# Attention, MLP and capacity MoE on one core: the turned product with v for five more pairs, and later stores and splits

## The chip, the cores and the metric

The kernel runs on 1 core of one Trainium2 chip, in one launch. The metric is the device time of that launch in microseconds (us), the median of several executions. TensorE is PE in the profile (PEld is its weight load), VectorE is DVE, ScalarE is ACT, GpSimd is POOL, and SyncE, which issues nearly all DMAs, is SP.

## The reference

Three stages follow each other. The change touches the first and the way in which weights of the second are prepared.

```python
# attention: 4 batches, 12 heads, 448 tokens, head size 64
q_n, k_n = rmsnorm(q, g_q), rmsnorm(k, g_k)
scores = q_n @ k_n.T / 8
attn = exp(scores - max(scores)); attn = attn / (sum(attn) + 1e-9)
x = attn @ v                       # to 1792 tokens x 768
# hardswish MLP, 768 -> 2048 -> 768; its weights arrive as 64-bit floats
h = x @ w_in;  g = h * clip(h + 3, 0, 6) / 6;  x = g @ w_out
# MoE: 8 experts of 224 tokens each, tokens assigned by capacity
out = relu(x @ w1[e]) @ w2[e]
```

## The kernel before, in words

Attention works on pairs of heads: 24 pairs, numbered i = 0 to 23, six of them (NP) to a batch. The order of all work is written out by hand: each piece is an event with a time in steps, 16 steps to a pair (`at(t + T_..., function, i)` with t = 16 i, near line 720), and the events are recorded in the order of these times. Between the events pieces of the first MLP product (`h`, L520) are laid in, but only once a batch is complete; so between the pairs of the first batch there are none, and the attention stands alone there.

The steps of a pair that matter here, with their lines:

- `sums`, `invert`, `norm` (L240 to L269): squares on ACT (`sq`), their sums on DVE (`st`, L249), the inverse root for two pairs at a time in 11 small DVE operations (L253 to L258), and the two scaled operands `xn` on POOL.
- `transp` (L286 to L298): PE turns `xn`; ACT and DVE make a high and a low part (`qh`, `kh`, `ql`, `kl`).
- `s1` (L309): scores for the maximum; DVE reduces them (`mx`, L312); `mt` (L318, L320) turns the maxima and DVE spreads them as `mr`.
- `sT` (L331): the turned scores minus the maximum; ACT takes the exponential into `ph` (L342).
- The product with v comes in two forms. `av` (L371) keeps queries on the rows: 32 small products of 66 columns for a pair, whose 65th column is the sum; DVE copies the sums (`scol`, L386), ACT the rest (`num`, L387), POOL divides (`normalize`, L392), and `xt` (L403 to L405) turns the result on PE and splits it on ACT and DVE. `pv` (L420) gives the turned result at once: 8 products of 448 columns. Its sums need more: `padd` (L413) adds blocks of `ph` in pairs on POOL, four operations of 448 columns; `psums` (L429) sums them on PE; the sums go out to memory, come back in another shape, are inverted on DVE (L444), go out again and come back spread over 64 rows (`rs_out`, `rs_in`, `r_out`, `r_in`, L435 to L454, five DMAs on SP); then POOL multiplies (`xmul`, L458), ACT takes the high part and POOL the low part (`xsplit`, L466 and L468).

The table `QMAJOR` names the pairs that use `av`. Within a pair I call A(i) the first score block (`sT` of parts 0 and 1, with `s1` parts 2 and 3 of pair i + 1) and B(i) the second (`sT` of parts 2 and 3, with `s1` parts 0 and 1 of pair i + 2).

`conv` (L147 to L171) narrows the 64-bit weights in 128-row units, 16 of `w_in` (one every 10 steps from step 20 on) and then 16 of `w_out` (one every 12 steps from step 180 on): one ACT operation (L138) and three DVE operations (L139 to L141) into the one buffer `cv`, then a store on SP (L171 for `w_in`, L169 for `w_out`). All PSUM tiles share eight banks under one tag, and every engine works its instructions off in the order in which they are recorded.

Of the kernel before, what the change touches and what calls it, by code (L numbers as in the profile page):

```python
# [21 lines left out]
def kernel(  # L22
# [15 lines left out]
    B, H, S, D = q.shape  # L38
# [7 lines left out]
    NP = H // 2  # L46
# [27 lines left out]
    T_AV = ((17, 18, 19.5, 20.5), (22, 23, 24.5, 25.5))  # L74
    T_NUM, T_XT, T_MLP = 28, 33, (37, 41, 41, 37)
    T_ADD, T_PV, T_SUM = (6, 13), (15.6, 15.62, 15.64, 15.66), 15.7
    T_RS, T_RL, T_REC, T_RO, T_RB, T_X, T_XH, T_XL = 19.5, 21.5, 24, 25.5, 28, 33, 35.5, 39.5
    GD, WD2, C_ST = 12, 8, 5
    QMAJOR = tuple(range(NP)) + (B * NP - 1,)
    T_CI, D_CI, T_CO, D_CO, T_CL = 20, 10, 180, 12, 14  # L80


# [52 lines left out]
    def narrow(lo, hi, v):  # L135

        vi = v.bitcast(I32)
        return (lambda: nc.scalar.activation(v, hi.bitcast(F32), AF.Copy, scale=2.0 ** -112),  # L138
                lambda: nc.vector.tensor_scalar(vi, vi, 3, None, op0=OP.logical_shift_left),  # L139
                lambda: nc.vector.scalar_tensor_tensor(vi, lo, 29, vi, op0=OP.logical_shift_right, op1=OP.bitwise_or),  # L140
                lambda: nc.vector.scalar_tensor_tensor(vi, hi, -2147483648, vi, op0=OP.bitwise_and, op1=OP.bitwise_or))  # L141
# [5 lines left out]
    def conv(key, part):  # L147

        out_, n = key
        rows = slice(n * 128, (n + 1) * 128)  # L150
        if part < 0:
            raw = rawp.tile([128, 768, 2], I32, name="wraw", bufs=2)
            if out_:
                nc.sync.dma_start(raw.rearrange("p f t -> p (f t)"), w_out.bitcast(I32)[rows, :])
            else:
                nc.sync.dma_start(raw.rearrange("p (c f) t -> p c (f t)", c=NC),
                                  w_in.bitcast(I32)[:, n * 256:(n + 1) * 256].rearrange("(c p) f -> p c f", p=128))
            RAW[key] = raw
            return
        if part == 0:  # L160
            raw = RAW[key]
            v32 = rawp.tile([128, 768], F32, name="cv", bufs=CB)
            RAW[key] = (v32, narrow(raw[:, :, 0], raw[:, :, 1], v32))
        v32, steps = RAW[key]
        if part < 4:
            steps[part]()
        elif part == C_ST:
            if out_:
                nc.sync.dma_start(wo32[rows, :], v32)  # L169
            else:  # L170
                nc.sync.dma_start(w32[:, rows].rearrange("(c p) f -> p c f", p=128), v32.rearrange("p (c f) -> p c f", c=NC))  # L171
# [551 lines left out]
    def at(t, fn, *args):  # L723
        events.append((t, len(events), fn, args))
# [7 lines left out]
    for i in range(NH // 2):  # L732
        t = 16 * i
# [11 lines left out]
        for c in range(NCH):  # L745
            at(t + (T_S1[c] if i else -24 + 0.1 * c), s1, i, c)
            at(t + T_ST[c], sT, i, c)
            if i in QMAJOR:
                for s in range(2):
# [3 lines left out]
        at(t + (T_MT if i else -21), mt, i)  # L753
        if i in QMAJOR:
            at(t + T_NUM, normalize, i)
# [13 lines left out]
    for u in range(NF if wide else 0):  # L769
        for out_, t in ((0, T_CI + D_CI * u), (1, T_CO + D_CO * u)):  # L770
            at(t - T_CL, conv, (out_, u), -1)
            for part in (0, 1, 2, 3, C_ST):
                at(t + part, conv, (out_, u), part)
    events.sort(key=lambda e: e[:2])
    ENDS = [8 * H * (b + 1) - 16 + T_MLP[b] for b in range(B)]
    now = 0
# [554 lines left out]
```

## Time and profile before

| | |
|---|---|
| median of 3 runs | 1217.49 us (1215.24 to 1219.66) |
| profiled execution, its own time | 1219.53 us |
| its span in the profile | 1217.7 us |
| mean granted TensorE clock | 0.978 |
| busy over the span | PE 94%, DVE 64%, ACT 45%, POOL 40% |
| chain that ended last | PE 62%, DVE 14%, DMA 9%, issue 6%, ACT 4%, POOL 2% |

The busy share is a mean over stages with different limits: attention with the first MLP product fills about the first 550 us, the rest belongs to the second MLP product, the routing and the experts. A line of the timeline gives start, length, engine, line, operation, output and inputs, how many were merged, and in brackets the idle time before with what ended it.

### The profile page before, as it was taken

The page shows a single profiled execution, that of the slowest core. Times are in us where ns is not written, and L with a number is a line of the kernel's source. Part 1 is how long each engine was busy: PE and PEld are TensorE (multiplying, and loading weights), DVE is VectorE, ACT ScalarE, POOL GpSimd, SP SyncE. Part 2 cuts the span into 40 slices and gives each one's busy share as a digit, 9 for nine tenths or more (in the row PEclk, how much of TensorE's full clock was granted, in tenths as well). Part 3 has the DMA queues.
Part 4 walks back from the last instruction along what each step waited for, and adds up shares of the span by engine and source line. Part 5 has one row for each costly group of instructions (what it writes and reads, how often), then busy time and mean ns, then how long its engine had stood idle before and what let it go on. Part 6 is the DMA issues. An engine that isn't in the chain of part 4 may idle for free.

```text
span 1217.7 us, 19761 instructions
## 1 busy us (share of the span) xinstructions
PE 1145.3 (94%) x7204; PEld 931.2 (76%) x7204; DVE 780.7 (64%) x1580; ACT 552.1 (45%) x1019; POOL 490.6 (40%) x362
## 2 busy tenths in 40 slices
PE   3988999999999999999979999999998799999997
PEld 2877656667676677787758787777778799999997
DVE  7887977767657665346893466666676675555550
ACT  3655646555454555446663111111123566555650
POOL 2222554754345432112352222222243677666640
PEclk9888999999999999999999999999999899999999
DMA  4355998977786866649895222222234688778731
GB/s 127 116 163 144 261 303 255 302 273 242 236 279 214 277 223 241 211 149 321 261 298 157 61 75 66 79 57 65 79 100 129 203 257 263 229 235 240 230 116 45
DMA packets 210708, 230.84 MB, mean 190 GB/s; under 512 B 24338, under 2 KB 183732, under 8 KB 210612
## 3 DMA queue, kind: packets, MB, share of 16 engines
q1 hardware_dynamic: 207284, 218.58, 58.3%
q0 software_dynamic: 3328, 11.01, 3.0%
q8 instruction: 56, 0.92, 0.3%
q14 instruction: 40, 0.33, 0.1%
HBM read 178.57 MB, written 50.98 MB: 189 GB/s over the span
## 4 chain that ended last, share of the span: by engine, by line
PE 62%; DVE 14%; DMA 9%; issue 6%; ACT 4%; POOL 2%; SPq 1%; POOLq 0%; DVEq 0%; ACTq 0%
PE y L1135 16%; PE h L520 10%; PE y L1283 8%; PE h L1219 5%; PE st L331 4%; PE av L420 3%; PE av L371 3%; PE h L1221 2%; PE sm L429 2%; PE rt L945 2%; DMA gr<-g_dr 1%; DMA wo_s<-wo 1%; PE s L309 1%; DVE C L940 1%; DMA we_s<-in_moe_w_dram 1%
## 5 line engine op out<-in xcount | busy, mean ns | idle before, releaser
L520 PE MATMUL h<-xh,w 128*128 128x448 f32 x768 | 240.3, 381 | 0.6 <-DVE mr L320 0.3
L520 PEld LDWEIGHTS h<-xh,w 128*128 128x128 f32 x768 | 144.8, 192 | 30.6 <-issue 14.3
L1078 POOL TENSOR_TENSOR g2l<-gr,g2h 128x512 fp32r<-128x512 f32 x60 | 79.1, 1319 | 207.1 <-ACT g2h L1076 159.8
L520 PE MATMUL h<-xl,w 128*128 128x448 f32 x384 | 145.7, 379 | 0.0
L312 DVE TENSOR_REDUCE mx<-s 112x1 f32<-112x448 f32 x192 | 105.9, 612 | 54.2 <-PE s L309 54.1
L1076 ACT ACTIVATE g2h<-gr 128x512 fp32r<-128x512 f32 x60 | 37.9, 631 | 207.1 <-PE y L1135 157.5
L1135 PE MATMUL y<-woh,g2l 128*128 128x512 f32 (+1 forms) x448 | 128.7, 349 | 1.0 <-POOL g2l L1078 1.0
L1135 PE MATMUL y<-woh,g2h 128*128 128x512 f32 (+1 forms) x448 | 128.1, 349 | 0.0
L1135 PE MATMUL y<-wol,g2h 128*128 128x512 f32 (+1 forms) x448 | 126.4, 346 | 0.0
L116 DVE TENSOR_TENSOR wel<-we_s,weh 128x768 fp32r<-128x768 f32 x59 | 80.6, 1372 | 61.5 <-ACT weh L115 59.2
L115 ACT ACTIVATE weh<-we_s 128x768 fp32r<-128x768 f32 x107 | 88.9, 842 | 59.3 <-DMA we_s<-in_moe_w_dram 41.1
L116 POOL TENSOR_TENSOR wel<-we_s,weh 128x768 fp32r<-128x768 f32 x48 | 95.5, 1991 | 46.7 <-ACT weh L115 36.0
L342 ACT ACTIVATE ph<-st 112x448 f32<-112x448 f32 x192 | 93.0, 544 | 46.9 <-PE st L331 46.0
L413 POOL TENSOR_TENSOR pa<-ph 112x448 f32<-112x448 f32 x68 | 85.8, 1282 | 53.6 <-ACT ph L342 53.4
L1219 PE MATMUL h<-xe,weh 128*128 128x448 f32 x318 | 101.4, 378 | 2.2 <-DVE xe L1170 2.2
L520 PEld LDWEIGHTS h<-xl,w 128*128 128x128 f32 x384 | 73.9, 192 | 10.8 <-issue 4.5
L1135 PEld LDWEIGHTS y<-woh,g2l 128*128 128x128 f32 x448 | 73.0, 190 | 10.9 <-POOL g2l L1078 1.3
L1135 PEld LDWEIGHTS y<-woh,g2h 128*128 128x128 f32 x448 | 73.0, 190 | 10.6 <-issue 1.4
L1135 PEld LDWEIGHTS y<-wol,g2h 128*128 128x128 f32 x448 | 72.6, 190 | 9.9 <-issue 0.2
L1221 PE MATMUL h<-xe,wel 128*128 128x224 f32 x318 | 77.2, 270 | 0.0
L1283 PE MATMUL y<-weh,hl 128*112 128x384 f32 x216 | 72.9, 338 | 0.0
L1283 PE MATMUL y<-weh,hh 128*112 128x384 f32 x216 | 72.8, 337 | 0.0
(256 smaller groups left out, 2493.4 us busy)
## 6 DMA issues: line engine op xcount, KB each, us to landing
we_s<-in_moe_w_dram SPq DMA_DIRECT2D x128, 384.0 KB
w<-w_hl SPq DMA_DIRECT2D x32, 768.0 KB
g_dr<-g SPq DMA_DIRECT2D x64, 224.0 KB
gr<-g_dr SPq DMA_DIRECT2D x52, 256.0 KB
wraw<-in_moe_w_in_dram SPq DMA_DIRECT2D x16, 768.0 KB
win_v<-w SPq DMA_DIRECT2D x32, 384.0 KB
w_hl<-w SPq DMA_DIRECT2D x16, 768.0 KB
wraw<-in_moe_w_out_dram SPq DMA_DIRECT2D x16, 768.0 KB
```

The lines of the kernel that those rows point to most:

```text
L115: nc.scalar.activation(hi, raw, AF.Copy)
L116: eng.tensor_tensor(lo, raw, hi.bitcast(F32), op=OP.subtract)
L312: mx = nc.vector.tensor_reduce(MX[i][:, s, c:c + 1], pp[s][:CP, :S], axis=AX.X, op=OP.max)
L331: nc.tensor.matmul(pp[s][:CP, :S], a[r], b[r], start=(n == 0), stop=(n == len(todo) - 1))
L342: nc.scalar.activation(e, pp[s][:CP, :S], AF.Exp)
L413: nc.gpsimd.tensor_tensor(PA[i, s, n], PP[i, s, 2 * n][0], PP[i, s, 2 * n + 1][0], op=OP.add)
L520: nc.tensor.matmul(p[:, :S], lhs[:, c], x[:, c], start=(n == 0), stop=(n == 3 * NC - 1))
L1078: eng.tensor_tensor(gl, g, gh.bitcast(F32), op=OP.subtract)
L1135: nc.tensor.matmul(pp[hf][:, :COLS[hf].stop - COLS[hf].start], a[:, f % QF], w[:, COLS[hf]], start=(f == 0 and n == 0), stop=(f == NF - 1 ...
L1219: mm = [lambda: nc.tensor.matmul(p[:, :4 * CP], wh[:, fo], x.rearrange("d k t -> d (k t)"), start=(c == 0), stop=(c == NC - 1), skip_group ...
L1221: lambda: nc.tensor.matmul(p[:, :2 * CP], wl[:, fo], x[:, 0], start=False, stop=False, skip_group_check=True)]
L1283: nc.tensor.matmul(p[:CP, :HW], a[:, f, tk], w[:, o], start=(f == 0 and n == 0), stop=(f == FB - 1 and n == 2))
```

## The change

```diff
-    T_RS, T_RL, T_REC, T_RO, T_RB, T_X, T_XH, T_XL = 19.5, 21.5, 24, 25.5, 28, 33, 35.5, 39.5
-    GD, WD2, C_ST = 12, 8, 5
-    QMAJOR = tuple(range(NP)) + (B * NP - 1,)
+    T_RS, T_RL, T_REC, T_RO, T_RB, T_X, T_XH, T_XL = 19.5, 21.5, 24, 25.5, 28, 34, 36.5, 40
+    GD, WD2, C_ST = 12, 8, 8
+    QMAJOR = (NP - 1, B * NP - 1)
...
-        elif part == C_ST:
+        else:
...
-            for part in (0, 1, 2, 3, C_ST):
+            for part in (0, 1, 2, 3):
                 at(t + part, conv, (out_, u), part)
+            at(t + (C_ST if out_ else 5), conv, (out_, u), 4)
```

Pairs 0 to 4 go from `av` to `pv`; pairs 5 and 23 keep `av`. For all pairs with `pv`, `xmul` and the high part move by one step, the low part by half a step. The store of a narrowed unit of `w_out` moves from 5 to 8 steps behind the unit's start; that of `w_in` stays at 5.

On PE, between the last `s1` product of B(1) and A(2), there stood before half of pair 0's `av` products of the second head; this is the order before:

```order
L309 MATMUL s_595<-kh,qh 112x448
L309 MATMUL s_596<-kh,qh 112x448
L371 MATMUL av<-vv_129,ph 112x66 x8
L331 MATMUL st<-qh,kh 112x448 x2
L331 MATMUL st<-qh,kl 112x448 x2
```

and this is the same place after the change:

```order
L309 MATMUL s_600<-kh,qh 112x448
L309 MATMUL s_601<-kh,qh 112x448
L420 MATMUL av<-ph,vv_131 64x448 x8
L429 MATMUL sm<-pa,ones_123 64x448 x4
L331 MATMUL st<-qh,kh 112x448 x2
L331 MATMUL st<-qh,kl 112x448 x2
```

All of pair 1's product with v and its sums now stand between B(1) and A(2); the 24 `av` products that stood between A and the next `mt` are gone.

On POOL in the same place, the operations of the first batch before:

```order
L269 TENSOR_TENSOR xn_425<-ld_q,st_2_249 112x2x4x64
L269 TENSOR_TENSOR xn_427<-ld_k,st_2_249 112x2x4x64
L269 TENSOR_TENSOR xn_612<-ld_q,st_2_430 112x2x4x64
L269 TENSOR_TENSOR xn_614<-ld_k,st_2_430 112x2x4x64
L392 TENSOR_TENSOR num<-num,scol 112x512
L269 TENSOR_TENSOR xn_789<-ld_q,st_2_430 112x2x4x64
```

and after:

```order
L269 TENSOR_TENSOR xn_429<-ld_q,st_2_249 112x2x4x64
L269 TENSOR_TENSOR xn_431<-ld_k,st_2_249 112x2x4x64
L413 TENSOR_TENSOR pa<-ph 112x448 x4
L269 TENSOR_TENSOR xn_609<-ld_q,st_2_438 112x2x4x64
L269 TENSOR_TENSOR xn_611<-ld_k,st_2_438 112x2x4x64
L413 TENSOR_TENSOR pa<-ph 112x448 x2
L458 TENSOR_TENSOR xn_t<-xn_t,rb 128x448
L413 TENSOR_TENSOR pa<-ph 112x448 x2
L466 TENSOR_TENSOR xl<-xn_t,xh 128x448
```

The adds of a pair's later parts stand right behind the two `xn` operations, which wait for `invert` where a new group of two pairs begins.

On SP, in the stage of the `w_out` units, the store moves behind the two DMAs of a pair's inverse sums (the numbers behind `dr` differ only because tiles are counted):

```order
 L506 DMA w_hl_109<-w 128x1536
-L169 DMA wo_97<-cv 128x768
-L448 DMA rec_dr_2798<-rs 112x8
-L454 DMA rb<-rec_dr_2798 64x448 x2
+L448 DMA rec_dr_2742<-rs 112x8
+L454 DMA rb<-rec_dr_2742 64x448 x2
+L169 DMA wo_97<-cv 128x768
 L531 DMA g_dr_62<-g 128x448
```

## Rows read from the trace of the kernel before

**Rows 1.** Busy by stretches: us; PE, PEld, DVE, ACT, POOL; clock; DMA share, GB/s.

```profile
37.00:120.00 83.00, 73.62 (x588) 63.03 (x587) 67.55 (x143) 46.16 (x91) 17.63 (x16) 0.86 0.49 134
...
120.00:183.00 63.00, 59.52 (x358) 40.69 (x358) 51.43 (x80) 35.06 (x63) 34.42 (x25) 0.97 0.94 276
...
74.00:80.00 6.00, 3.49 (x23) 2.05 (x23) 5.66 (x18) 2.63 (x6) 1.20 (x2) 0.87 0.47 133
80.00:85.00 5.00, 5.00 (x28) 4.54 (x29) 2.09 (x6) 1.32 (x3) 1.90 (x2) 0.50 0.60 171
```

**Rows 2.** Timeline of PE: the starts of A(1), A(3) and A(6).

```profile
34.91 0.37 PE L331 MATMUL st<-qh,kh 64*112 64x448 f32 x2
...
64.51 0.46 PE L331 MATMUL st<-qh,kh 64*112 64x448 f32 x2
...
115.44 0.72 PE L331 MATMUL st<-qh,kh 64*112 64x448 f32 x2
```

**Rows 3.** Groups by line, 54 to 68 us, one pair: busy us, mean ns, idle.

```profile
L371 PE MATMUL av<-vv,ph 112*112 112x66 f32 x64 | 6.9, 261 | 0.0
...
L403 PE MATMUL t<-ident,num 112*128 112x112 f32 x4 | 0.6, 273 | 0.0
```

**Rows 4.** Timeline of PE: av at the lower clock, pv and its sums later.

```profile
79.16 0.71 PE L309 MATMUL s<-kh,qh 64*112 64x448 f32 x2 [2.25 <-DVE mr L320]
79.80 3.25 PE L371 MATMUL av<-vv,ph 112*112 112x66 f32 x16
...
333.02 3.23 PE L420 MATMUL av<-ph,vv 112*64 112x448 f32 x16
336.08 1.67 PE L429 MATMUL sm<-pa,ones 112*64 112x448 f32 x8
```

**Rows 5.** Timeline of the other engines, first batch: prices of single operations.

```profile
34.90 0.98 ACT L342 ACTIVATE ph<-st 112x448 f32<-112x448 f32 x2 [0.33 <-PE st L331]
...
61.88 2.22 DVE L312 TENSOR_REDUCE mx<-s 112x1 f32<-112x448 f32 x4 [0.57 <-PE s L309]
...
76.15 0.17 DVE L253 TENSOR_SCALAR st<-st 112x32 f32<-112x32 f32 x1
...
78.49 0.62 DVE L320 TENSOR_TENSOR mr<-t,place 128x448 fp32r<-128x448 f32 x1
...
97.64 0.38 SPq L171 DMA_DIRECT2D w<-cv  x1
...
100.99 0.91 ACT L138 ACTIVATE cv<-wraw 128x768 f32<-128x768 f32 x1 [0.91 <-DMA w<-cv]
...
104.24 0.68 DVE L298 SCALAR_TENSOR_TENSOR ql<-t,gq,qh 128x448 fp32r<-128x448 f32 x1
...
104.83 1.27 DVE L249 TENSOR_REDUCE st<-sq 112x8 f32<-112x512 f32 x2
...
111.25 1.04 POOL L269 TENSOR_TENSOR xn<-ld_q,st 112x512 f32<-112x512 f32 x1 [11.90 <-DVE st L258]
```

**Rows 6.** Groups by line, 30 to 118 us: busy us, mean ns, idle before.

```profile
L140 DVE SCALAR_TENSOR_TENSOR cv<-wraw,cv 128x768 int32<-128x768 int32 x8 | 7.6, 952 | 0.0
...
L141 DVE SCALAR_TENSOR_TENSOR cv<-wraw,cv 128x768 int32<-128x768 int32 x7 | 7.0, 997 | 0.1
...
L139 DVE TENSOR_SCALAR cv<-cv 128x768 int32<-128x768 int32 x8 | 4.7, 584 | 3.8 <-ACT cv L138 3.8
```

**Rows 7.** The same view, 300 to 480 us.

```profile
L413 POOL TENSOR_TENSOR pa<-ph 112x448 f32<-112x448 f32 x32 | 38.1, 1213 | 41.4 <-ACT ph L342 41.3
...
L140 DVE SCALAR_TENSOR_TENSOR cv<-wraw,cv 128x768 int32<-128x768 int32 x11 | 13.6, 1236 | 0.1
L141 DVE SCALAR_TENSOR_TENSOR cv<-wraw,cv 128x768 int32<-128x768 int32 x11 | 12.9, 1177 | 0.2
```

**Rows 8.** One line's operations, 250 to 400 us: count, least, median, most ns.

```profile
L140 DVE SCALAR_TENSOR_TENSOR cv<-wraw,cv x10: 947/958/2646, 251.9 to 394.6; 128x768 int32<-128x768 int32 x10
```

**Rows 9.** Waits: SP, 300 to 560 us; all engines, 183 to 305 us: us, times, longest.

```profile
SPq L169 <- DVE cv L141: 17.9, 6, 7.7
...
POOL xn_t L458 <- DMA rb<-rec_dr: 28.3, 6, 10.8
```

## The prediction
> **What bounds the kernel now.** I read the busy times by stretches first, then the timeline of the first batch, then the groups that give prices. From 37 to 120 us, while the first batch's attention stands alone, PE is busy 73.62 of 83 us at a granted clock of 0.86 and DVE 67.55, while POOL has only 17.63 [rows 1]. So two engines nearly share the bound there, and the reader should see in the timeline how they take turns. Where two pairs' inverse roots fall due, DVE is late with mr and the PE instruction behind it idles 2.25 us [rows 4]; in that stretch, 74 to 80 us, PE is busy 3.49 of 6 us and DVE 5.66, and right behind it, from 80 to 85 us, the granted clock is 0.50, the lower of the two levels, 1.2 GHz [rows 1]. In the other pairs PE itself is the bound, filled by the av products. From 120 to 183 us PE is busy 59.52 of 63 us and the DMA engines 0.94 of the time [rows 1]: there PE and the transfers are the limit, and nothing of this change removes work.
>
> **What pairs 0 to 4 lose and gain on PE.** A pair loses 64 av passes, 6.9 us, and the turn of its result, 0.6 [rows 3], and gets the 16 passes of pv and 8 of the sums, 3.23 and 1.67 us, as a later pair shows them at full clock [rows 4]. That is 2.6 us less a pair, 13.0 for five. This is the far end of the gain, since it counts only where PE is the bound.
>
> **What they add elsewhere.** POOL gets four adds of 1.21 us [rows 7], a multiplication and a subtraction, and loses a division: about five operations more a pair. DVE loses some small copies and a split. Five small DMAs a pair go to SP, which is hardly used in the first batch; behind its waits for their landing stand only loads that are ordered 14 steps or more before their use and the store of the next w_in unit. The new order matters more than the sums: pv and the sums stand between B(i) and A(i+1), so A(i+1) waits for the exponentials of B(i) and for the adds made of them. Before, av ran a pair behind and waited for nothing.
>
> **The path, pair by pair.** The prices: an add 1.21 [rows 7]; two exponentials 0.98, four maxima 2.2, mr 0.62, ql or kl 0.68, two square sums 1.27, an xn 1.04, the inverse root 2.3 (from 76.15 to the start of mr) [rows 5]; narrowing steps 0.58, 0.95 and 1.00 [rows 6]; from a store's issue to the next unit's ACT step 3.35, from 97.64 to 100.99, and that step 0.91 [rows 5]. The maxima of A(i) end 3.2 us after its start, 1.0 for the first products and 2.2 on DVE; behind the last add the sums need 0.4.
>
> - A(1), 34.91 before [rows 2]. B(0)'s exponentials end at 35.88 [rows 5]; two adds 2.4 and 0.4: 38.7, so 3.8 later than before.
> - A(2). Maxima at 41.9; ql, square sums, kl, one narrowing step and the inverse root, 5.5: 47.4. POOL's next two xn wait for that root and the adds stand behind them: 2.1 and 2.4; with 0.4, 52.3.
> - A(3), 64.51 before [rows 2]. After the root two narrowing steps and mr, 2.6: 50.0; the store, 53.3; ACT 54.2; the next unit on DVE with the maxima between its steps, 4.7: 58.9; store and ACT again, 63.2; the last two exponentials of B(2) stand behind that ACT step, 64.2; adds and sums 2.8: 67.0, 2.5 later than before.
> - A(4). Maxima 70.2; ql, kl, square sums, three narrowing steps and the root, 7.5; I add 1.0 for operands that ACT delivers late, because a narrowing step stands ahead of them: 78.7; two xn, two adds, the sums, 4.9: 83.6.
> - A(5). Maxima 86.8, mt 0.3 and B(4) 2.0: 89.1; the last exponential behind a narrowing step at 90.9; adds and sums 2.8: 93.7.
> - A(6), 115.44 before [rows 2]. Pair 5 keeps av, so no pv stands here, and pair 4's last 16 av passes are gone. DVE must first end a unit, 0.7, then the maxima: 97.6; 7.5, 1.0 and mr 0.6: 106.7. That is 8.7 us earlier.
>
> Two corrections. The idle time before A(6) stays, so the lower clock will follow again, but the 16 av passes that met it, 3.25 us [rows 4] against 1.7 at full clock (a quarter of 6.9 [rows 3]), are replaced by other products that meet it: I give back 1.5. And POOL, at 21% busy from 37 to 120 us [rows 1], goes to about 60% with some five operations of 1.2 us more in each of five pairs. The two narrowing steps that read two operands, 952 and 997 ns there [rows 6], take 1236 and 1177 in a stage with many adds [rows 7]: 0.46 us a unit. Four units lie on the path above: 1.9 us. The lower end is 0, as in today's rows; the upper is rows 8, below.
>
> Sum: -8.7 + 1.5 + 1.9 = -5.3 us.
>
> The Trainium skill, "SBUF — State Buffer", section "Who interferes with whom", says that a VectorE instruction with two SBUF inputs and a GpSimd one that reads SBUF share a port, and that whoever comes first holds it for the whole instruction while the other blocks; it speaks against this change. By that rule, if each of the eight two-input steps on the path met an add, 8 x 1.21 = 9.7 us would stand in place of 1.9, and the sum would be +2.5. The rows agree in kind, with a most of 2646 ns against a median of 958 [rows 8], and not in frequency.
>
> **The other edits.** xmul one step later: POOL waits there for rb anyway, 28.3 us in six waits from 183 to 305 us [rows 9], and no add changes place with it, so it runs when rb lands as before. The high part now stands behind kh on ACT; a gain, if any, hides under the products of the MLP on PE. The later w_out stores take SP out of waits of 17.9 us for the narrowing [rows 9]; what stands behind them are loads ordered well ahead. If the store landed only after the next unit's ACT step is due, it would hold the exponentials behind that step; four steps of 1.0 us or more (80 steps from A(1) to A(6) take 80.5 us [rows 2]) against 3.35 to land [rows 5] leave a little room. I take 0 for these together, between -1.5 and +1.5.
>
> **Rivals.**
> 1. *The port decides.* If the eight two-input steps all meet POOL at the worst seen, 1.7 us over the median [rows 8], that is 13.6 us in place of 1.9: -8.7 + 1.5 + 13.6 = +6.4, 1223.9 us. From 0.9 us a step on it takes the whole gain (7.2 over 8), from 1.4 on it is slower by more than can be told apart. For it: POOL triples. Against it: the mean of such steps later is only 0.2 to 0.3 over.
> 2. *The stage behind takes it back.* From 120 to 183 us the DMA share is 0.94 [rows 1]; if its transfers can't begin earlier, the gain is waited away there: 1217.5. For it: units are paced by steps, and the stage reads what they store. Against it: their loads begin earlier too, as the DMA share before is 0.49 [rows 1].
> 3. *PE's whole saving counts,* because the adds always lie under something: -13.0, 1204.5. Against it: A(2) and A(4) above hang on DVE and POOL, not on PE.
>
> That the change doesn't do what it says is ruled out by the recorded order.
>
> **The numbers.** The sum is against the profiled execution, 1219.53 us, which lies 2.0 above the median; the same 5.3 taken from the median of 1217.49 gives 1212.2 us. About 0.3%, 3.65 us, is what a measurement can tell from no change. My forecast has a chance of 0.58, its own range 1208 to 1216.5: 0.42 of it beyond that bound, 0.13 within and 0.03 in a tail on the other side. Rival 1 has 0.15, rival 2 0.19, rival 3 0.08. Faster: 0.42 + 0.08 = 0.50; same: 0.13 + 0.19 = 0.32; slower: 0.03 + 0.15 = 0.18. The range, 1205 to 1220, takes in rival 2 wholly and the near half of rivals 1 and 3.
>
> **What would show it.** In the new profile: L371 with a sixth of its count before 240 us (one pair of six); A(1) at 38 to 40, A(3) at 66 to 69, A(6) at 105 to 109 us; PE idle ahead of the sums on pa; the narrowing steps before 118 us at a mean near 1.2 us; after 120 us the same work, some 5 us earlier. It is wrong if A(6) comes no earlier than 112, if the two-input steps pass 1.9 us, or if A(6) is early and the start of the second MLP product is not.

## The result and the profile after

| | before | after |
|---|---|---|
| median of the runs, us | 1216.37 (1213.49 to 1219.66, 4 runs) | 1229.38 (1226.16 to 1231.11, 4 runs) |
| profiled execution, its span, us | 1219.53, 1217.7 | 1226.16, 1224.3 |
| start of A(6) on PE, us | 115.44 | 116.15 |
| start on DVE of mr for pair 6, which A(6) needs, us | 110.94 | 119.21 |

The changed kernel is slower: the ratio is 1.0118, with an interval of 1.0093 to 1.0143, some 13 us. The forecast was 5.3 us faster, with a range up to 1220; the time lies 9 us beyond it, and beyond rival 1. The profiled pair differs by only 6.6 us. Of the two, the profile before is near its slowest run and the one after is its fastest; traces are used below for what happens, and the repeated runs for how much it costs.

The busy times of the two stretches, against [rows 1]:

```profile
37.00:120.00 83.00, 63.51 (x359) 33.82 (x357) 61.23 (x121) 46.30 (x87) 40.65 (x33) 0.88 0.51 141
120.00:183.00 63.00, 60.30 (x345) 44.61 (x347) 50.84 (x80) 34.22 (x62) 34.77 (x27) 0.86 0.88 252
```

PE is busy 63.51 us in place of 73.62, DVE 61.23 in place of 67.55, and POOL 40.65 in place of 17.63. Neither PE nor DVE has more to do, yet the work ends later: the stretch is now filled with waiting. The starts of A(1) to A(6), on PE's timeline, and the product of A(6) that waits for mr:

```profile
38.65 0.46 PE L331 MATMUL st<-qh,kh 64*112 64x448 f32 x2
...
54.98 0.71 PE L331 MATMUL st<-qh,kh 64*112 64x448 f32 x2
...
68.91 0.46 PE L331 MATMUL st<-qh,kh 64*112 64x448 f32 x2
...
91.56 0.71 PE L331 MATMUL st<-qh,kh 64*112 64x448 f32 x2
...
104.52 0.46 PE L331 MATMUL st<-qh,kh 64*112 64x448 f32 x2
...
116.15 1.13 PE L331 MATMUL st<-qh,kh 64*112 64x448 f32 x2 [0.26 <-ACT ph L342]
...
119.89 0.46 PE L331 MATMUL st<-mr,minus 64*112 64x448 f32 x2 [2.19 <-DVE mr L320]
```

The forecast was 38.7, 52.3, 67.0, 83.6, 93.7 and 106.7. The first is right; A(2) is 2.7 us late and A(3) 1.9, then 6.0 more are lost up to A(4) and 2.9 up to A(5). A(6) begins at 116.15, but from 117.7 us on it stands before its product with mr. DVE ends mr at 119.83; the forecast had it end at 106.7, with A(6) right behind. So 13.1 us are lost by then. (The expectations below count A(6) from 120.5 us in the changed kernel. That is its second block, behind the wait; the times of mr are the safer comparison.) Where the time went, the chain of work that ended last shows, from 36 to 125 us (start, us, what); these are all its DMAs:

```profile
61.06 2.34 DMA sum_dr<-rb
63.42 4.87 DMA rs<-sum_dr
...
84.51 6.06 DMA rec_dr<-rs
...
93.00 4.71 DMA sum_dr<-rb
97.77 4.11 DMA rs<-sum_dr
```

2.34 + 4.87 + 6.06 + 4.71 + 4.11 = 22.1 us of the small transfers that carry a pair's sums out and their inverses back. In the same stretch before, the chain has a single transfer, the store of a narrowed unit, 3.3 us. The 6.06 leads by little: it holds SP, which sends the next pair's sums at 93.00 us, and ACT has had these ready since 92.29 (91.66 and 0.63 long), over the adds and PE; that path is only 0.7 us shorter. At the far end of the transfers stand engines that work in order: DVE before the reciprocal and POOL before the multiplication. ACT's wait is for a transfer of another kind, the store of a narrowed unit, which SP could issue only at 81.45 us, when DVE had ended it. DVE, POOL and ACT, in that order:

```profile
68.31 0.20 DVE L444 RECIPROCAL rs<-rs 112x8 f32<-112x8 f32 x1 [6.04 <-DMA rs<-sum_dr]
...
74.16 2.21 DVE L312 TENSOR_REDUCE mx<-s 112x1 f32<-112x448 f32 x4
...
101.90 0.20 DVE L444 RECIPROCAL rs<-rs 112x8 f32<-112x8 f32 x1 [2.41 <-DMA rs<-sum_dr]
```

```profile
73.61 1.13 POOL L458 TENSOR_TENSOR xn_t<-xn_t,rb 128x448 f32<-128x448 f32 x1 [5.64 <-DMA rb<-rec_dr]
...
83.98 1.04 POOL L269 TENSOR_TENSOR xn<-ld_q,st 112x512 f32<-112x512 f32 x1 [4.37 <-DVE st L258]
...
85.98 3.83 POOL L413 TENSOR_TENSOR pa<-ph 112x448 f32<-112x448 f32 x2
...
110.90 1.14 POOL L458 TENSOR_TENSOR xn_t<-xn_t,rb 128x448 f32<-128x448 f32 x1 [7.33 <-DMA rb<-rec_dr]
```

```profile
84.65 0.89 ACT L138 ACTIVATE cv<-wraw 128x768 f32<-128x768 f32 x1 [3.49 <-DMA w<-cv]
```

And on PE, what comes of it:

```profile
76.42 0.45 PE L318 MATMUL t<-ident,mx 112*128 112x112 f32 x1 [4.11 <-DVE mx L312]
...
88.07 3.56 PE L429 MATMUL sm<-pa,ones 112*64 112x448 f32 x4 [3.81 <-POOL pa L413]
```

From 62.3 to 68.3 us DVE stands before an operation of 0.20 us. Behind it stand the maxima of B(2), three narrowing steps, two square sums and only then the maxima of A(3), at 74.16 us. So the inverse root is late, POOL's two xn, which wait for it, and the adds behind them; and PE, which needs the maxima and the adds, idles 4.11 and 3.81 us. This accounts for the 6.0 us between A(3) and A(4). The maxima end 7.5 us after A(3) starts (76.37 less 68.91), where the forecast had 3.2: 4.3 lost. From the start of the first xn to A(4) it takes 7.6 us (91.56 less 83.98), where the forecast had 4.9: 2.7 lost, half of it in the two adds, which take 3.83 us and not 2.4. The 1.0 us that the forecast had added for late operands isn't needed. The narrowing groups, 30 to 118 us, against [rows 6]:

```profile
L141 DVE SCALAR_TENSOR_TENSOR cv<-wraw,cv 128x768 int32<-128x768 int32 x7 | 8.6, 1232 | 0.1
L140 DVE SCALAR_TENSOR_TENSOR cv<-wraw,cv 128x768 int32<-128x768 int32 x7 | 8.2, 1175 | 0.1
```

They take 0.23 us more each, as forecast (0.46 a unit). On the average this isn't where the time went, though at 87.06 us, beside the two slow adds, both steps take 1.76 us and more. And the av products from 30 to 240 us, 384 passes and 45.6 us before, are a sixth:

```profile
L371 PE MATMUL av<-vv,ph 112*112 112x66 f32 x64 | 11.3, 360 | 0.0
```

### The profile page after: what moved, and what is told of

Read it like the earlier page. It is cut to its first block, busy times and chain, and to the rows that moved or that the text cites. A ratio compares the mean times of both kernels' runs of the same rounds, so it can differ in the third digit from the quotient of the medians.

```text
span 1224.3 us, 19364 instructions
## 1 busy us (share of the span) xinstructions
PE 1138.6 (93%) x6984; PEld 904.0 (74%) x6984; DVE 787.5 (64%) x1565; ACT 554.4 (45%) x1019; POOL 520.0 (42%) x387
## 4 chain that ended last, share of the span: by engine, by line
PE 60%; DVE 16%; DMA 11%; issue 6%; ACT 3%; POOL 2%; SPq 1%; POOLq 0%; DVEq 0%; ACTq 0%
PE y L1136 16%; PE h L520 11%; PE y L1284 8%; PE h L1220 5%; PE st L331 4%; PE av L420 3%; PE h L1222 3%; PE sm L429 2%; PE rt L946 2%; DMA wo_s<-wo 2%; DMA rec_dr<-rs 1%; DVE mx L312 1%; PE av L371 1%; DMA w_hl<-w 1%; DMA g_dr<-g 1%
## 5 line engine op out<-in xcount | busy, mean ns | idle before, releaser
L520 PE MATMUL h<-xh,w 128*128 128x448 f32 x768 | 236.6, 376 | 3.9 <-DVE mr L320 3.8
L520 PEld LDWEIGHTS h<-xh,w 128*128 128x128 f32 x768 | 141.8, 188 | 33.6 <-issue 13.5
L413 POOL TENSOR_TENSOR pa<-ph 112x448 f32<-112x448 f32 x88 | 109.0, 1259 | 51.9 <-ACT ph L342 51.9
L116 DVE TENSOR_TENSOR wel<-we_s,weh 128x768 fp32r<-128x768 f32 x59 | 85.5, 1458 | 57.5 <-ACT weh L115 57.4
L458 POOL TENSOR_TENSOR xn_t<-xn_t,rb 128x448 f32<-128x448 f32 x22 | 26.6, 1211 | 119.0 <-DMA rb<-rec_dr 119.0
```

The source lines that it names most:

```text
L116: eng.tensor_tensor(lo, raw, hi.bitcast(F32), op=OP.subtract)
L413: nc.gpsimd.tensor_tensor(PA[i, s, n], PP[i, s, 2 * n][0], PP[i, s, 2 * n + 1][0], op=OP.add)
L520: nc.tensor.matmul(p[:, :S], lhs[:, c], x[:, c], start=(n == 0), stop=(n == 3 * NC - 1))
```

## The experiments

Ratios are of the time to that of the kernel before, run on the same chip, with a 95% interval; "under the changed kernel" compares them with 1.0118. The start of mr for pair 6 (on DVE; A(6) needs it) is 110.94 us before and 119.21 after.

### The change in its three parts

```diff
@@ e1_q_only, on the kernel before
-    QMAJOR = tuple(range(NP)) + (B * NP - 1,)
+    QMAJOR = (NP - 1, B * NP - 1)
@@ e2_x_only, on the kernel before
-    T_RS, T_RL, T_REC, T_RO, T_RB, T_X, T_XH, T_XL = 19.5, 21.5, 24, 25.5, 28, 33, 35.5, 39.5
+    T_RS, T_RL, T_REC, T_RO, T_RB, T_X, T_XH, T_XL = 19.5, 21.5, 24, 25.5, 28, 34, 36.5, 40
@@ e3_store_only, on the kernel before
-            for part in (0, 1, 2, 3, C_ST):
+            for part in (0, 1, 2, 3):
                 at(t + part, conv, (out_, u), part)
+            at(t + (8 if out_ else 5), conv, (out_, u), 4)
```

> Only the pairs are changed, with the old times of the parts of x and of the w_out stores. Theory A (the loss is made in the first batch, by waits that the new path brings): nearly all of the loss is here, 8 to 13 us over the kernel before, and A(6) starts at 118 to 122 us as in the changed kernel. Theory B (the shifts of the parts of x and of the stores cost it, in the batches behind): A(6) late too, but the time is within 4 us of the kernel before.

> Only the parts of x come later, pairs 0 to 4 as before. Theory A: within 2 us of the kernel before. Theory B: 4 us or more slower, with ACT or POOL waits behind the parts of x from 183 us on that the kernel before does not have.

> Only the w_out stores come three steps later. Theory A: within 2 us of the kernel before; SP's wait for the last narrowing step (17.9 us in six waits before) is gone. Theory B: 4 us or more slower, with ACT waiting at its narrowing step (line 138) for the stored tile in the w_out stage.

Measured: the pairs alone 1.0081 (1.0055 to 1.0106), the parts of x 1.0006 (0.9987 to 1.0026), the stores 1.0023 (1.0003 to 1.0042). Of a median of 1212.75 us for the kernel before in this set that is 9.8, 0.7 and 2.8 us; together 13.3, about what the whole change costs. So theory A carries most. It put the stores within 2 us; they cost 2.8, with an interval from 0.4 to 5.1, so some cost is likely and its size is open. On ACT in that run, then on PE:

```profile
485.03 0.91 ACT L138 ACTIVATE cv<-wraw 128x768 f32<-128x768 f32 x1 [2.10 <-DMA wo<-cv]
```

```profile
487.58 0.28 PE L670 MATMUL lg<-wo_t,wgs 128*8 128x256 f32 x1 [1.72 <-DVE wo_t L662]
```

The store now lands after the next unit's ACT step is due; the exponentials and copies behind that step wait with it, and PE idles 1.72 us. At this step ACT has no wait for `wo` in the kernel before, and two here, 2.7 us in all. That the stores' cost is these waits is argued from the trace, and wasn't tried.

### Order alone: a later trip, adds ahead of xn, products behind A

```diff
@@ e4_late_trip, on the changed kernel; o = 6 for pairs 0 to 4, else 0
-            for d, fn in ((T_SUM, psums), (T_RS, rs_out), (T_RL, rs_in), (T_REC, rec), (T_RO, r_out), (T_RB, r_in), (T_X, xmul)):
+            for d, fn in ((T_SUM, psums), (T_RS, rs_out), (T_RL, rs_in)):
                 at(t + d, fn, i)
-            at(t + T_XH, xsplit, i, False)
-            at(t + T_XL, xsplit, i, True)
+            for d, fn in ((T_REC, rec), (T_RO, r_out), (T_RB, r_in), (T_X, xmul)):
+                at(t + d + o, fn, i)
+            at(t + T_XH + o, xsplit, i, False)
+            at(t + T_XL + o, xsplit, i, True)
@@ e5_adds_first, on the changed kernel
-        at(t + T_NORM, norm, i)
+        at(t + (T_NORM + 3.5 if 2 < i < NP + 2 else T_NORM), norm, i)
@@ e6_pv_behind_A, on the changed kernel; T_SUM to T_XL also 6 later for pairs 0 to 4
-                at(t + T_PV[c], pv, i, c)
+                at(t + ((17, 18, 19.5, 20.5) if i < NP else T_PV)[c], pv, i, c)
```

> The changed kernel, but in pairs 0 to 4 the reciprocal, both DMAs behind it, the multiplication and the split come six steps later. Theory A1 (DVE's reciprocal and POOL's multiplication wait in order for the DMA round trip of the sums, 6.0 and 5 to 7 us at a time, and hold the maxima, the narrowing and the adds behind them): those waits shrink under 1 us each, A(4) starts at 85 to 88 us instead of 91.6, A(6) at 109 to 114 instead of 120.5, and the time comes 5 to 9 us under the changed kernel. Theory A2 (the adds behind two xn on POOL, which wait for the inverse root, hold the sums and A): the waits for the round trip vanish, but A(6) stays at 118 to 121 and the time within 3 us of the changed kernel.

> The changed kernel, with the two normalizing operations (xn) of pairs 3 to 7 ordered on POOL behind a pair's last adds, 3.5 steps later, so that no add waits for an inverse root. Theory A2 (adds behind xn hold the sums and with them A): PE's waits of 2.1 and 3.8 us for the adds vanish, A(6) starts at 113 to 117 us in place of 120.5 and the time is 4 to 8 us under the changed kernel. Theory C (what costs is the lower clock: PE now idles before 120 us, and from 120.7 to 137.2 us, where the first MLP begins and PE has no idle time, it runs at 0.50, which the kernel before does not): A(6) may come earlier, but so long as 120 to 137 us stays at the lower clock the time is within 3 us of the changed kernel.

> The changed kernel, with pv and the sums of pairs 0 to 4 behind A(i+1) instead of ahead of it, as the av products stood, and all that follows the sums six steps later. Theory A2: A no longer waits for adds or exponentials, A(6) at 106 to 112 us, the time 5 to 12 us under the changed kernel. Theory C: A(6) earlier too, and the time falls by more than 4 us only if the stretch at the lower clock ends before about 120 us; if PE is at 0.50 from A(6) on for 15 us again, less than 4 us.

Measured: 1.0107 (1.0082 to 1.0131), 1.0122 (1.0083 to 1.0162) and 1.0147 (1.0103 to 1.0190): none differs from the changed kernel by more than can be told. Yet each took its own wait away. With the late trip no reciprocal waits, and A(4) comes at 87.25 us and mr of pair 6 at 113.71, 5.5 earlier; but only 2.9 of that is left at the end of the first MLP product (ACT's `r` at 153.28 in place of 156.20). With the adds first, PE waits for no add, as at the sums of pair 3, and mr of pair 6 is no earlier, because the next wait is in their place:

```profile
69.28 0.20 DVE L444 RECIPROCAL rs<-rs 112x8 f32<-112x8 f32 x1 [6.23 <-DMA rs<-sum_dr]
...
102.68 0.20 DVE L444 RECIPROCAL rs<-rs 112x8 f32<-112x8 f32 x1 [4.40 <-DMA rs<-sum_dr]
...
119.60 0.62 DVE L320 TENSOR_TENSOR mr<-t,place 128x448 fp32r<-128x448 f32 x1
```

```profile
84.67 1.67 PE L429 MATMUL sm<-pa,ones 112*64 112x448 f32 x8
```

So A2 alone falls, and A1 by order alone gains no time. In the third, reciprocals wait 11.8 us in three times and ACT 12.9 us in five for stored units.

### The lower clock

A granted clock of 0.86 from 120 to 183 us, where the kernel before has 0.97 [rows 1], suggested another cause. Two kernels keep PE busy with products of constants whose results are overwritten.

```diff
@@ e8_fill, on the changed kernel, ahead of the turned maxima and of the sums
+        for _ in range(n):
+            nc.tensor.matmul(p[:64, :S], ones64, place[:CP].rearrange("p c k -> p (c k)"), start=True, stop=True)
@@ e12_fill_half, half as many
+        for k in range(n):
+            nc.tensor.matmul(p[ROWS[k % 2], :S], ones64, place[:CP].rearrange("p c k -> p (c k)"), start=True, stop=True)
```

> The changed kernel with 58 more products (448 columns, 0.2 us each) of constants, whose results are overwritten: 6, 16 and 8 ahead of the turned maxima of pairs 3, 4 and 6, and 8, 16 and 4 ahead of the sums of pairs 1, 3 and 4, where PE idles 1.3, 4.1, 2.0, 2.2, 3.8 and about 1 us now. No wait of another engine is changed. Theory C: the granted clock from 120 to 137 us is 0.9 or more in place of 0.50, and the time is 4 to 8 us under the changed kernel, though PE has 11.7 us more to do. Theories A1 to A3 (the waits themselves cost): the products fill idle time or lengthen the path, the time is the same or up to 4 us over the changed kernel.

> The filling products again, at a size that fits the idle times: 28 in pairs over the two halves of the columns, so that one takes 0.4 us as pv's do (the ones before took 0.77), 11 us in all. Theory C (the lower clock): the granted clock from 80 to 140 us comes to 0.95 or more and the time falls 4 us or more under the changed kernel. Theories A: within 4 us of the changed kernel or slower, whatever the clock does.

Measured: 1.0278 (1.0243 to 1.0312) and 1.0150 (1.0115 to 1.0184). In the first a product took 0.77 us and not 0.2, since all went to the same half of the columns; my size was wrong, and its total says nothing. With alternating halves, in the second, it took 0.41. But in the first the clock did what was wanted for a while. The stretch from 120 us on, in e8_fill:

```profile
120.00:148.00 28.00, 24.99 (x169) 15.92 (x167) 20.12 (x41) 14.08 (x27) 10.21 (x10) 1.00 0.63 169
```

and of the changed kernel:

```profile
120.00:137.00 17.00, 17.00 (x89) 14.84 (x91) 13.55 (x20) 6.52 (x13) 9.63 (x8) 0.52 0.87 230
```

Three marks follow each other in both kernels: mr of pair 6, PE's turned maxima of pair 7, and mr of pair 7. Between them both do the same work, but for three products of A(6) that the changed kernel has ahead of the first mark. In e8_fill, at full clock up to 148.4 us,

```profile
135.17 0.62 DVE L326 TENSOR_TENSOR mr<-t,place 128x448 fp32r<-128x448 f32 x1
143.88 0.26 PE L324 MATMUL t<-ident,mx 112*128 112x112 f32 x1
149.96 0.61 DVE L326 TENSOR_TENSOR mr<-t,place 128x448 fp32r<-128x448 f32 x1
```

and in the changed kernel:

```profile
119.21 0.62 DVE L320 TENSOR_TENSOR mr<-t,place 128x448 fp32r<-128x448 f32 x1
133.52 0.39 PE L318 MATMUL t<-ident,mx 112*128 112x112 f32 x1
134.29 0.61 DVE L320 TENSOR_TENSOR mr<-t,place 128x448 fp32r<-128x448 f32 x1
```

PE gets to the maxima 8.7 us behind mr of pair 6 at full clock and 14.3 at the lower one, 5.6 later; mr of pair 7 follows 14.8 and 15.1 us behind, 0.3 later. So up to there the lower clock costs next to nothing: in e8_fill PE is early, and DVE waits 3.3 us for ACT's narrowing step, which waits for a store. Further on the pair is no test, since e8_fill itself runs at 0.50 from 148.4 to 158.5 us. In the second kernel the granted clock from 37 to 120 us came to 0.95, and from 120 to 137 it was 0.52 again, so it doesn't test that stretch either; up to 120 us theory C gets no support. What speaks most clearly against C is a run further on, e14_rest, without the trip and the adds. It has the lower clock as long,

```profile
112.00:131.00 19.00, 17.64 (x89) 15.39 (x91) 15.53 (x25) 7.17 (x13) 10.68 (x8) 0.50 0.86 224
```

and its time is 1.0019. C falls as the main cause.

### Without the trip, without the adds, without both

```diff
@@ e7_no_adds, on the changed kernel, pairs 0 to 4, and no padd for them
-                nc.tensor.matmul(p[r, :S], ones64, PA.pop((i, s, n)), start=(n == 0), stop=(n == 1))
+                    for c in (2 * n, 2 * n + 1):
+                        nc.tensor.matmul(p[r, :S], ones64, PP[i, s, c][0], start=(c == 0), stop=(c == NCH - 1))
@@ e9_no_trip, on the changed kernel
+            trip = ((T_RS, rs_out), (T_RL, rs_in), (T_REC, rec), (T_RO, r_out), (T_RB, r_in))
-            for d, fn in ((T_SUM, psums), (T_RS, rs_out), (T_RL, rs_in), (T_REC, rec), (T_RO, r_out), (T_RB, r_in), (T_X, xmul)):
+            for d, fn in ((T_SUM, psums),) + (trip if i >= NP else ()) + ((T_X, xmul),):
@@ e10_rec_direct, the same, with this at T_REC for pairs 0 to 4
+        nc.vector.reciprocal(RB[i], RB[i])
@@ e11_no_trip_no_adds: e7 and e9 together
@@ e14_rest: e11 with the old times of the stores and the parts of x
@@ e15_bound: e14 with pv as in e6, the sums and the parts of x 6 later
```

> The changed kernel, with the sums of pairs 0 to 4 made on PE from all four parts of the exponentials (16 passes in place of 8, 1.7 us more a pair) and no adds on POOL there. Theory A3 (POOL's adds cost: their waits, and the shared port that slows the narrowing): POOL is busy some 25 us less before 120 us, lines 140 and 141 fall back to 0.95 and 1.0 us, and the time is 5 to 10 us under the changed kernel. Theory C: PE is busier (8 us more), so the lower clock from 120 us on should shorten or go; the time falls by 4 to 8 us with it, and by under 3 us where it stays.

> The changed kernel, with the round trip of the sums of pairs 0 to 4 left out: no small DMAs and no reciprocal, POOL multiplies by the sums themselves (so the division is left out of the computation in these pairs; the adds and the sums stay). Theory A1 (the round trip blocks in order: DVE at the reciprocal, POOL and behind it ACT at the multiplication and the split, SP at its waits for landings, with the stores of the narrowed w_in behind them): A(6) at 108 to 113 us, ACT's wait at line 138 for a stored tile nearly gone, the time 6 to 10 us under the changed kernel. Theory A4 (A waits anyway, for exponentials and adds that now stand between B(i) and A(i+1), and nothing covers it): A(6) at 115 or later and the time within 4 us of the changed kernel.

> As the run without the round trip, but whole in its computation: DVE inverts the broadcast sums, 128x448, in one operation, in pairs 0 to 4. Its price isn't in any row: between 0.6 us (mr, of the same size) and 11 us (56 times the 0.2 us of the 112x8 one). Theory A1: if it takes under 2 us, A(6) at 109 to 115 us and 4 to 9 us under the changed kernel; at 4 us or more DVE, with five of them before 120 us, takes it back. Theory A4: no better than the changed kernel at any price.

> Neither the round trip nor the adds in pairs 0 to 4 (the sums come from PE with 16 passes, and POOL multiplies by them; the division is left out there). If A1 and the adds explain the loss between them, A(6) is at 104 to 109 us, as forecast, and the time is at or under that of the kernel before (up to 6 us under). Theory A4: A(6) at 110 or later, since A still waits for the exponentials, and the time 3 us or more over the kernel before.

> Neither trip nor adds in pairs 0 to 4, as before (the division is left out there), now with the old times of the stores and the parts of x. If the parts add up, 6.0 us over the kernel before less 3.5: 1 to 4 us over it, and adds and trip together made some 7 of the 9.8 us that the pairs cost. If it comes out at the kernel before or under, they made all of it.

> As the run before it, and pv and the sums of pairs 0 to 4 behind A(i+1), the parts of x six steps later: no trip, no adds, and A waits for nothing of its own pair's product. If PE's time were the bound in the first batch (the forecast's far end), this shows the gain: PE has about 1 us less a pair, and A(6) at 103 to 108 us, 3 to 7 us under the kernel before. If the pace there is set by DVE, ACT and the stores of the narrowed units, A(6) stays at 107 us or later and the time within 3 us of the kernel before.

Where the trip is left out without e10's inverse (e9, e11, e14, e15), the division is left out with it in pairs 0 to 4: POOL multiplies by the sums themselves. These kernels show what a wait is worth and compute something else.

| run | ratio to before | mr of pair 6, us |
|---|---|---|
| changed kernel | 1.0118 (1.0093 to 1.0143) | 119.21 |
| no adds (e7) | 1.0105 (1.0073 to 1.0138) | 116.01 |
| no trip (e9) | 1.0088 (1.0057 to 1.0119) | 116.37 |
| one inverse on DVE (e10) | 1.0113 (1.0076 to 1.0149) | 114.50 |
| neither (e11) | 1.0049 (1.0024 to 1.0074) | 110.27 |
| neither, old times (e14) | 1.0019 (1.0003 to 1.0036) | 112.67 |
| neither, old times, behind A (e15) | 1.0020 (1.0002 to 1.0037) | 112.03 |

The trip alone is worth 0.0030 and the adds alone 0.0013, both within what the intervals leave open; together they are worth 0.0069, 8 us, which the intervals do separate. How the 8 us divide, and whether one covers for the other, the ratios can't show: 0.0030, 0.0013 and 0.0069 are each uncertain by some 0.004. The chains suggest that they do cover for each other. Without the trip the chain from 36 to 125 us runs over the adds and the xn ahead of them:

```profile
85.09 3.74 POOL pa L413 x2
...
97.29 3.25 POOL xn L269 x2
```

There, too, the two-input narrowing steps take 1397 and 1361 ns (L140, L141; 30 to 118 us) in place of 1175 and 1232, 2.5 us more over 14 steps, which takes back a part of what the trip gives. Without the adds the chain runs over the trip:

```profile
60.59 2.34 DMA sum_dr<-rb
62.95 4.66 DMA rs<-sum_dr
...
91.37 5.45 DMA sum_dr<-rb
96.88 2.19 DMA rs<-sum_dr
```

Without both, in e11, over the stores of the narrowed units:

```profile
51.78 3.32 DMA w<-cv
60.57 3.26 DMA w<-cv
87.30 3.48 DMA w<-cv
97.03 3.28 DMA w<-cv
```

That chain has 13.3 us of stores, 35.1 of DVE and 27.7 of PE. In e14, whose first batch differs only by the times of the parts of x, it has one store of 3.1 us, 33.2 us of DVE and 38.2 of PE. So no single engine is the bound; they take turns. Even with nothing new in the way the time is 2.3 us over the kernel before (0.4 to 4.4), and the saving of PE doesn't show. (This kernel saves PE only some 1 us a pair: 7.5 us less 3.23 for pv and twice 1.67 for sums of 16 passes [rows 3, 4].)

One theory is left, A4: A waits for the exponentials that now stand between B(i) and A(i+1). By the expectations e9 and e11 speak for it, since mr of pair 6 comes at 116.37 and 110.27 us and the times are 3.6 us under the changed kernel and 5.9 over the kernel before. But e15, in which A waits for nothing of its own pair's product, comes to 1.0020, and e14, in which it does, to 1.0019. So that wait is worth nothing that can be told.

In e10 one inverse of 128x448 takes 2.94 us, in five of them 14.7 us on DVE, and the time is that of the changed kernel.

### Versions that compute everything

```diff
@@ e13_no_adds_late: e7 and e4 together, old times of the stores and the parts of x
@@ e16_behind_no_adds: e7 and e6 together, old times of the stores and the parts of x
@@ e17_later_trip, e16 with o = 9 for pairs 0 to 4 from rec on
-            for d, fn in ((T_REC, rec), (T_RO, r_out), (T_RB, r_in), (T_X, xmul)):
-                at(t + d + 6, fn, i)
+                at(t + d + 9, fn, i)
@@ e18_latest_trip, the same with 11
```

> No adds in pairs 0 to 4 (sums from PE), the reciprocal and what follows it six steps later, and the old times of the stores and the parts of x; whole in its computation. If the late trip frees the engines as much as leaving it out does (theory A1 with order as its cause), the time is within 3 us of the run that has neither, less the 3.5 us of the stores and parts of x: 0 to 4 us over the kernel before. If DMA traffic or SP's waits remain the cost, 5 to 8 us over.

> The same order, whole in its computation: pv and sums (from PE) behind A(i+1), the trip six steps later, no adds, old times of the stores and the parts of x. Best case, with the trip's waits off the path: at the kernel before or up to 4 us under it. If the trip still blocks SP, DVE or POOL in order: 3 to 8 us over it.

> As the run with the products behind A and no adds, whole in its computation, and the reciprocal and what follows it another three steps later (nine in all). There DVE still waited 12.8 us in four times for the sums to land (4.2 us at most), with the narrowing steps and maxima behind it. If these waits are on the path, they fall under 2 us in all and the time by 2 to 6 us, under the kernel before. If something else sets the pace there (products on PE, the units' stores), the waits go and the time stays within 2 us.

> The same with the reciprocal and what follows five steps later still than in the run with the products behind A (eleven in all). DVE's waits near zero; if they were on the path, 3 to 7 us under the kernel before, and no worse than nine steps; if not, within 2 us of it, or slower where the multiplication and the split now meet the next pair's square sums and exponentials.

Measured: 1.0033 (1.0011 to 1.0055), 1.0004 (0.9983 to 1.0025), 1.0133 (1.0108 to 1.0159) and 1.0089 (1.0063 to 1.0115). e16 is level with the kernel before; no version beats it. The last two were misses, and telling ones: DVE no longer waits for the sums, as wanted, and the time rises by 16 and 10 us against e16. In e16 the DMA of pair 4's inverses leaves SP at 123.14 us, ahead of the first loads for the MLP at 126.90. In the last two it stands behind them (in e18_latest_trip the loads at 121.22, the inverses at 127.46); in e17_later_trip:

```profile
122.95 4.08 SPq L179 DMA_DIRECT2D win_v<-w  x3
127.12 1.47 SPq L453 DMA_DIRECT2D rec_dr<-rs  x1
```

ACT's split waits for it (6.0 us; 4.1 in e18_latest_trip), with the exponentials behind, and in e17_later_trip PE for the adds made of them:

```profile
137.85 0.58 ACT L473 ACTIVATE xh<-xn_t 128x448 fp32r<-128x448 f32 x1 [6.03 <-POOL xn_t L463]
```

```profile
141.99 1.75 PE L434 MATMUL sm<-pa,ones 112*64 112x448 f32 x2 [5.87 <-POOL pa L414]
```

A later trip for pairs 0 to 3 alone wasn't tried.

## Why the prediction was wrong

- **Right.** A(1) at 38.7 us (38.65). The weight of the narrowing steps, 0.46 us a unit (0.223 and 0.235). That PE loses work: 10.1 us less busy from 37 to 120 us, though at 120 us the changed kernel is also less far. That A would wait for the adds behind xn was in the walk too, at too low a price.
- **The step that failed: the walk from A(3) to mr of pair 6.** It gave 39.7 us (67.0 to 106.7); the changed kernel takes 50.9 (68.91 to 119.83). Two things were wrong in it. First, it carried the adds, the inverse roots, the narrowing and their stores, and no transfer of the trip. The forecast said that DVE "loses some small copies and a split", and of the five DMAs a pair that they go to SP, behind whose waits stand only loads and a store. But at the far end of the transfers stand engines: DVE with the reciprocal, POOL with the multiplication, ACT with the split behind that. Steps that fit batches with MLP work between the pairs don't fit the first one. So the maxima of A(3) ended 7.5 us after its start and not 3.2. Second, the adds were walked at too low a price: two xn, two adds and the sums took 7.6 us up to A(4) and not 4.9, and up to A(5) two xn stood ahead of the adds (99.04 to 101.35 us) where the walk has none.
- **What each is worth.** The same stretch takes 46.6 us without the trip (e9, 70.44 to 116.99), 47.3 without the adds (e7, 69.31 to 116.63), and 41.2 and 41.8 without both (e11, 69.68 to 110.89; e14, 71.45 to 113.29), each in one profiled execution. So e9, which leaves out just what the walk left out, is still 7 us over the walk; only without both does the stretch come within some 2 us of it.
- **The price of a transfer.** The only one that the walk used was a store's, 3.35 us to the next step [rows 5]. The five on the chain took 2.3 to 6.1. The Trainium skill, "DMA: Bandwidth & Descriptors", section "Anatomy of one DMA — SWDGE (gpsimd) path", gives a fixed cost of about 2.0 us for DMAs issued from GpSimd. These are issued from SP, and only the shortest of them comes near.
- **The other edits.** They were taken as 0, within 1.5 us. Together they measure 3.5, of which the 0.7 of x can't be told from nothing; the 2.8 of the stores are clear of nothing by little, and the trace shows the way that the forecast named and set aside: the store lands after the next unit's ACT step is due.
- **The clock.** 1.5 us were given back for it. It has a price at single places: at a granted clock of 0.55 (91 to 93.5 us) the two blocks of A(4) start 1.9 us apart, those of A(5), at 1.00, 1.1. But e14, with 19 us at 0.50, is only 2.3 us over the kernel before, so it isn't the main cause. The 1.5 themselves weren't measured.
- **Rival 1** named the right side and a near time (1223.9), and not the cause: the two-input steps grew by 0.2 us, not by 0.9, and without POOL's adds they fall to 1.0 and 1.1 us (lines 140 and 141) while the time hardly moves. The rule of the Trainium skill that stood beside it, "SBUF — State Buffer", section "Who interferes with whom", would have made it 9.7 us; steps that meet an add do take 1.76 us (lines 140 and 141 beside the adds of 85.98 us), but few do. What the rival didn't name is the other side: those two adds took 3.83 us and not 2.4, on the way to A(4). **Rival 2**: the stage behind gave back some of the loss, 8.3 us at mr of pair 6 and 6.0 at mr of the last pair, but set no floor. **Rival 3**: the runs without trip and adds show no gain from PE's saving, but they save only some 1 us a pair of the 2.6.
- What would have shown it wrong was named: A(6) no earlier than 112 us. It begins at 116.15.

What stays open: how the 8 us divide between trip and adds, and how the last 2 us of the pairs' part arise (e14), which are near what can be told apart at all.

## What to carry to other kernels

When a path is moved to a place where the engines have less other work, walk every transfer of it to the instruction that waits at its far end, and count what stands behind that instruction in order; an operation of 0.2 us can hold an engine for 6. If a run leaves out just what your walk forgot and is still far from the walk, the walk has a second fault: here e9 was 7 us over it. If taking one wait away gains nothing, take two away together before dropping the theory: here they were worth 0.0030 and 0.0013 alone, neither to be told from nothing, and 0.0069 together. And less busy time on the busiest engine is no gain where turns between engines set the pace.

## What was not expected of the hardware

- Products with 64 output columns took 0.21 us a pass when they alternated between the two halves, and 0.38 when all went to one half (busy time by passes, 5.8 by 28 and 21.5 by 56). The filling products ahead of the sums, first of e8_fill, then of e12_fill_half (passes, busy us, mean ns of one; the passes overlap, so the mean is no price):

```profile
L319 PE MATMUL sm<-place,ones 112*64 112x448 f32 x56 | 21.5, 539 | 0.0
```

```profile
L319 PE MATMUL sm<-place,ones 112*64 112x448 f32 x28 | 5.8, 539 | 0.0
```

- An inverse of 128x448 took 2.94 us on DVE, against 0.62 for a multiplication of that size and 0.20 for an inverse of 112x8 (the group of e10_rec_direct, 30 to 118 us):

```profile
L447 DVE RECIPROCAL rb<-rb 128x448 f32<-128x448 f32 x5 | 14.7, 2942 | 0.0
```

- From mr of pair 6 to mr of pair 7 it took 15.1 us at a granted clock of 0.55 (119 to 134 us, changed kernel) and 14.8 at 0.97 (135 to 149, e8_fill), though PE came 5.6 us later to the maxima between them. From 120 to 137 us PE was busy all the time, at 0.52.
